# Attention on one core: keys loaded in rows of eight, a first group in pieces, copies as words, and two routes that alternate by unit

## The chip, the cores and the metric

The kernel runs on one core of a Trainium2 chip. The time is device microseconds of one launch; the median of three runs before the change is 1265.33 us (1265.04 to 1265.5). One more execution was taken with the hardware profiler; everything said of stages and engines comes from it.

## The reference

Softmax attention over 512 independent heads (16 x 32), with 192 query rows, 1024 keys and a head width of 128, all in bf16:

```
B, H, Sq, Sk, D = 16, 32, 192, 1024, 128

def reference(q, k, v):
    scale = q.shape[-1] ** -0.5
    scores = jnp.einsum("bhqd,bhkd->bhqk", q, k) * scale
    p = _softmax(scores, axis=-1)
    return jnp.einsum("bhqk,bhkd->bhqd", p, v)
```

K and V are 134.2 MB each, Q and the output 25.2 MB each; all of it passes through the DMA engines once.

## The kernel before

**Tiling.** Heads are taken in groups of 16 (`G`), 32 groups in all. A group is eight pairs of heads, and a pair is three units of 128 query rows: rows 0 to 127 of head a, rows 0 to 127 of head b, and the last 64 rows of both side by side. The third kind of unit (`k3 == 2`) runs as two matmuls of 64 columns on two halves of the array (`tile_position`). There are 24 units in a group and 768 in the program; unit u of the text is u % 3 == k3.

**A unit's way.** TensorE makes the scores of all 1024 keys into PSUM (`s_ps`, L215, or L222 and L228 for the third unit): two matmuls of 512 columns, stationary operand from `qt`, moving operand from `kt`. VectorE copies them, scaled and negated, to `ss` in SBUF and takes the row's extreme on the way (L300). Then one of two routes follows:

- `R_W`: GpSimd subtracts the extreme and writes bf16 to `x_sb` (L188). TensorE transposes `x_sb` in eight blocks (L244) into `pt_ps`. ScalarE applies exp while it copies PSUM to `pt_sb` (L367). No row sum exists then, so TensorE makes it along with P times V: beside each of the eight matmuls with V (L267) stands one with a column of ones (L270), the same stationary operand again.
- `R_EA`: ScalarE applies exp first and accumulates the row sum in the same instruction (L356). TensorE transposes (L244), ScalarE copies PSUM to `pt_sb` unchanged (L369), and P times V needs no ones.

`ROUTES=(R_W, R_W, R_EA)` is indexed by u % 3, so both full units of a pair go by `R_W` and the third, split unit always by `R_EA`; its matmuls with V are L273 and L275, and the lines for ones on the split unit never run.

**Order.** Each engine has its own hand-written program and waits on semaphores. TensorE does in step s: scores of unit s+1, transposes of unit s-4, P times V of unit s-7. Three steps are a pair. `s_ps` and `pt_ps` have two buffers each, `x_sb` four.

**Keys.** `kt` holds K transposed, one key after another; a block of the transpose takes every eighth column, so that block t holds keys t, t+8, t+16 and so on, which is how V lies in `vs` (partition p holds the eight keys 8p to 8p+7, 2 KB in a row):

```
ins = pe.transpose(PT[:, t, :], X[:, t: SK: KT_TILES], ident[:])
```

**Loads and stores.** All DMAs are issued by SyncE (SP), in order, on one queue. For a group: K with a transpose in flight (L141, 4 MB), Q likewise (L144, 0.75 MB), V as it is (L149, 4 MB), and for the output three stores (L158, L163, L164, 0.75 MB). Two groups are held at once. The program's start loads groups 0 and 1; then, for each g, come the loads of g+2 and the stores of g. The load of K waits until the scores of group g are done (`s_qk`), that of V until its P times V is done (`s_pv`), the stores until its last pair is normalised (`s_on`).

Of the kernel before, what the change touches and what calls it, by code (L numbers as in the profile page):

```python
# [5 lines left out]
BF16 = mybir.dt.bfloat16  # L6
F32 = mybir.dt.float32
# [5 lines left out]
R_W = 2  # L13


def _attention_kernel(nc, q, k, v, out, G=16, NS=2, LAGS=(2, 4, 5, 7), ROUTES=(R_W, R_W, R_EA)):
    B, H, SQ, D = q.shape
    SK = k.shape[2]
    assert D == 128 and SK == 1024 and SQ == 192, (D, SK, SQ)
# [43 lines left out]
    with ExitStack() as es:  # L63
# [6 lines left out]
        def sem(name):  # L70
            return es.enter_context(nc.semaphore(name))

        kt = sb("kt", [128, NS, G * SK], BF16)
        qt = sb("qt", [128, NS, G * SQ], BF16)
        vs = sb("vs", [128, NS, G, KT_TILES, 128], BF16)
        ob = sb("ob", [128, NSO, PPG, 4, 128], BF16)
# [5 lines left out]
        rinv = sb("rinv", [128, 2, 4], F32)  # L82
        ones = sb("ones", [128, 128], BF16)
        ident = sb("ident", [128, 128], BF16)
        s_ps = [ps("s_ps%d" % i, [128, SK], F32) for i in range(2)]
        pt_ps = [ps("pt_ps%d" % i, [128, KT_TILES, 128], BF16) for i in range(2)]
        o_ps = [ps("o_ps%d" % i, [128, 4, 128], F32) for i in range(2)]
        s_setup = sem("s_setup")
        sxk = [sem("sxk%d" % i) for i in range(NS)]
        sxq = [sem("sxq%d" % i) for i in range(NS)]  # L90
        svl = [sem("svl%d" % i) for i in range(NS)]
        sst = [sem("sst%d" % i) for i in range(NSO)]
        s_qk = sem("s_qk")
        s_max = sem("s_max")
# [17 lines left out]

        O_SLOT = (0, 2, 1)

        def load_cnt(g):
            return 16 * (g // NS + 1)

        def store_cnt(g):
            return 48 * (g // NSO + 1)
# [12 lines left out]

        @block.sync
        def _(e):
            def loads(g):
                s = g % NS
                last_u = (g - NS + 1) * UPG - 1
                h0 = g * G
                if g >= NS:
                    e.wait_ge(s_qk, last_u + 1)  # L140
                e.dma_start_transpose(  # L141
                    kt[:, s], kf[h0:h0 + G].rearrange("g k d -> (g k) d")
                ).then_inc(sxk[s], 16)
                e.dma_start_transpose(  # L144
                    qt[:, s], qf[h0:h0 + G].rearrange("g k d -> (g k) d")
                ).then_inc(sxq[s], 16)
                if g >= NS:
                    e.wait_ge(s_pv, last_u + 1)
                e.dma_start(  # L149
                    vs[:, s], vf[h0:h0 + G].rearrange("g (p t) d -> p g t d", t=KT_TILES)  # L150
                ).then_inc(svl[s], 16)

            def stores(g):
                so = g % NSO
                e.wait_ge(s_on, (g + 1) * PPG)
                h0 = g * G
                og = of[h0:h0 + G]
                e.dma_start(  # L158
                    og[:, 0:128, :].rearrange("h p d -> p h d"),
                    ob[:, so].rearrange("p pg (x y) d -> p (pg x) (y d)", y=2)[:, :, 0:128],  # L160
                ).then_inc(sst[so], 16)
                oab = og[:, 128:192, :].rearrange("(pg x) p d -> x p pg d", x=2)
                e.dma_start(oab[0], ob[0:64, so, :, 1, :]).then_inc(sst[so], 16)  # L163
                e.dma_start(oab[1], ob[64:128, so, :, 1, :]).then_inc(sst[so], 16)  # L164

            for g in range(min(NS, NGR)):
                loads(g)
            for g in range(NGR):
                if g + NS < NGR:
                    loads(g + NS)  # L170
                stores(g)
            for so in range(min(NSO, NGR)):
                n_uses = len(range(so, NGR, NSO))
                e.wait_ge(sst[so], 48 * n_uses)

        @block.gpsimd
# [21 lines left out]
        def _(pe):  # L198
            def qk(u):
                pr, k3, g, pg = unit_info(u)  # L200
                s = g % NS
                if u % UPG == 0:
                    pe.wait_ge(sxk[s], load_cnt(g))
                    pe.wait_ge(sxq[s], load_cnt(g))
                if u >= 2:
                    pe.wait_ge(s_max, u - 1)
                S = s_ps[u % 2]
                a = 2 * pg
                b = 2 * pg + 1
                ins = None  # L210
                for c in range(2):
                    cs = slice(512 * c, 512 * c + 512)
                    if k3 < 2:
                        x = a if k3 == 0 else b
                        ins = pe.matmul(  # L215
                            S[:, cs],
                            qt[:, s, x * SQ: x * SQ + 128],
                            kt[:, s, x * SK + 512 * c: x * SK + 512 * c + 512],
                            start=True, stop=True,
                        )  # L220
                    else:
                        pe.matmul(  # L222
                            S[0:64, cs],
                            qt[:, s, a * SQ + 128: a * SQ + 192],
                            kt[:, s, a * SK + 512 * c: a * SK + 512 * c + 512],
                            start=True, stop=True, tile_position=(0, 0),
                        )
                        ins = pe.matmul(  # L228
                            S[64:128, cs],
                            qt[:, s, b * SQ + 128: b * SQ + 192],  # L230
                            kt[:, s, b * SK + 512 * c: b * SK + 512 * c + 512],
                            start=True, stop=True, tile_position=(0, 64),
                        )
                ins.then_inc(s_qk, 1)

            def tr(u):
                wait_x(pe, u)
                if u >= 2:
                    wait_evac(pe, u - 2)
                X = x_sb[:, u % NX, :]  # L240
                PT = pt_ps[u % 2]
                ins = None
                for t in range(KT_TILES):
                    ins = pe.transpose(PT[:, t, :], X[:, t: SK: KT_TILES], ident[:])  # L244
                ins.then_inc(s_tr, 1)

            def pv(u):
                pr, k3, g, pg = unit_info(u)
                s = g % NS
                if u % UPG == 0:  # L250
                    pe.wait_ge(svl[s], load_cnt(g))
                wait_evac(pe, u)
                if k3 == 0 and pr >= 2:
                    pe.wait_ge(s_on, pr - 1)
                O = o_ps[pr % 2]
                PTS = pt_sb[:, u % NPT]
                sl = O_SLOT[k3]
                a = 2 * pg
                b = 2 * pg + 1
                ins = None  # L260
                with_rs = route(u) == R_W
                for t in range(KT_TILES):
                    first = t == 0
                    last = t == KT_TILES - 1
                    if k3 < 2:
                        x = a if k3 == 0 else b
                        ins = pe.matmul(O[:, sl, :], PTS[:, t, :], vs[:, s, x, t, :],  # L267
                                        start=first, stop=last, skip_group_check=True)
                        if with_rs:
                            ins = pe.matmul(O[:, 3, sl: sl + 1], PTS[:, t, :], ones[:, 0:1],  # L270
                                            start=False, stop=last, skip_group_check=True)
                    else:
                        pe.matmul(O[0:64, sl, :], PTS[:, t, 0:64], vs[:, s, a, t, :],  # L273
                                  start=first, stop=last, skip_group_check=True, tile_position=(0, 0))
                        ins = pe.matmul(O[64:128, sl, :], PTS[:, t, 64:128], vs[:, s, b, t, :],  # L275
                                        start=first, stop=last, skip_group_check=True, tile_position=(0, 64))
                        if with_rs:
                            pe.matmul(O[0:64, 3, sl: sl + 1], PTS[:, t, 0:64], ones[:, 0:1],
                                      start=False, stop=last, skip_group_check=True, tile_position=(0, 0))
                            ins = pe.matmul(O[64:128, 3, sl: sl + 1], PTS[:, t, 64:128], ones[:, 0:1],  # L280
                                            start=False, stop=last, skip_group_check=True, tile_position=(0, 64))
                ins.then_inc(s_pv, 1)
# [12 lines left out]
        def _(dve):  # L295
            def rowmax(u):
                dve.wait_ge(s_qk, u + 1)
                if u >= NSS:
                    wait_x(dve, u - NSS)
                dve.tensor_scalar(  # L300
                    ss[:, u % NSS, :], s_ps[u % 2][:], -scale, None, ALU.mult, ALU.min,
                    accum_out=nb[:, u % NSS: u % NSS + 1],
                ).then_inc(s_max, 1)

# [43 lines left out]
        def _(act):  # L348
# [13 lines left out]
            def evac(u):  # L362
# [3 lines left out]
                if route(u) == R_W:  # L366
                    act.activation(pt_sb[:, u % NPT], pt_ps[u % 2][:], ACT_FN.Exp, scale=-1.0).then_inc(s_eva, 1)  # L367
                else:
                    act.activation(pt_sb[:, u % NPT], pt_ps[u % 2][:], ACT_FN.Copy).then_inc(s_eva, 1)  # L369

            for step in range(NU + L_EV + 1):
                u = step - L_EV
# [43 lines left out]
```

## Time and profile before

| | us |
|---|---|
| median of three runs | 1265.33 |
| span of the profiled execution (its own time; no other is recorded of it) | 1263.1 |
| TensorE matmul busy | 1234.2 |
| VectorE busy | 1102.0 |
| ScalarE busy | 1048.6 |
| GpSimd busy | 960.4 |
| first score matmul starts | 21.0 |
| last store issued | 1259.06 |

The mean granted TensorE clock is 0.999 of full speed. Busy time of TensorE is not TensorE at its peak: matmuls are pipelined, and their records overlap. The DMA engines moved 321.9 MB, 255 GB/s on average, of which K, Q and the output go in packets of 256 B. The share of the DMA engines in the page's slices stands at nine tenths or more from the first to the 38th of 40 slices. Instructions of the engines are themselves fetched by DMA: 164 packets of 16 KB, one in 7.7 us.

### The profile page before, as it was taken

How to read it: one execution, taken by the hardware profiler on the slowest of the kernel's cores; microseconds unless marked ns; L12 is line 12 of the kernel's file. 1: busy time of each engine (PE TensorE's matmuls, PEld its weight loads, DVE VectorE, ACT ScalarE, POOL GpSimd, SP SyncE). 2: the span in 40 equal slices, each digit the busy share in tenths (PEclk: the TensorE clock that was granted, in tenths of full speed). 3: DMA queues.
4: the chain of work that ended last, by engine and by line, in shares of the span. 5: the costliest groups of instructions: out<-in, count | busy, mean ns of one | idle time of the engine just before them, and what ended most of it. 6: DMA issues, size and time to landing. Idle time of an engine off the chain costs nothing.

```text
span 1263.1 us, 48658 instructions
## 1 busy us (share of the span) xinstructions
PE 1234.2 (98%) x20480; PEld 1009.4 (80%) x20480; DVE 1102.0 (87%) x2304; ACT 1048.6 (83%) x1281; POOL 960.4 (76%) x518
## 2 busy tenths in 40 slices
PE   3999999999999999999999999999999999999997
PEld 1888888888888888888888888888888888888886
DVE  2889888898988989898898988889898898989885
ACT  1888888888888888888888888888888888888886
POOL 2778777777877778787777877777787777878774
PEclk9999999999999999999999999999999999999999
DMA  9999999999999999999999999999999999999941
GB/s 288 268 261 240 278 280 266 288 270 245 254 269 261 279 233 255 281 275 262 261 230 272 271 276 268 252 251 272 272 267 281 253 263 252 271 261 281 244 118 27
DMA packets 790743, 321.89 MB, mean 255 GB/s; under 512 B 724992, under 2 KB 724992, under 8 KB 790528
## 3 DMA queue, kind: packets, MB, share of 16 engines
q1 hardware_dynamic: 790528, 318.78, 108.8%
q8 instruction: 164, 2.69, 0.8%
q14 instruction: 51, 0.42, 0.1%
HBM read 134.22 MB, written 25.17 MB: 126 GB/s over the span
## 4 chain that ended last, share of the span: by engine, by line
PE 97%; SPq 1%; DMA 1%; ACT 0%; issue 0%; DVE 0%; ACTq 0%
PE pt_ps L244 33%; PE o_ps L267 24%; PE s_ps L215 18%; PE o_ps L273 11%; PE s_ps L222 9%; SPq L141 1%; DMA vs<-in_v_dram 1%; PE o_ps L270 1%; PE o_ps L275 1%; SPq L144 0%; PE s_ps L228 0%; ACT x_sb L356 0%; ACT pt_sb L367 0%; DVE ob L330 0%; DVE rinv L327 0%
## 5 line engine op out<-in xcount | busy, mean ns | idle before, releaser
L188 POOL TENSOR_TENSOR x_sb<-ss,nb 128x1024 bf16<-128x1024 f32 x512 | 959.7, 1895 | 288.9 <-PE pt_ps L244 266.8
L300 DVE TENSOR_SCALAR_CACHE_REDUCE ss<-s_ps 128x1024 f32<-128x1024 f32 x768 | 938.5, 1222 | 140.5 <-PE s_ps L215 110.8
L244 PEld LDWEIGHTS pt_ps<-ident,x_sb 128*128 128x128 bf16 x6144 | 487.1, 148 | 203.3 <-issue 105.4
L367 ACT ACTIVATE pt_sb<-pt_ps 128x1024 bf16<-128x1024 bf16 x512 | 521.0, 1018 | 41.9 <-PE pt_ps L244 41.8
L244 PE MATMUL pt_ps<-ident,x_sb 128*128 128x128 bf16 x6144 | 520.7, 228 | 0.2 <-ACT pt_sb L367 0.2
L267 PE MATMUL o_ps<-vs,pt_sb 128*128 128x128 bf16 x4096 | 403.0, 217 | 0.3 <-DMA vs<-in_v_dram 0.3
L369 ACT ACTIVATE pt_sb<-pt_ps 128x1024 bf16<-128x1024 bf16 x256 | 262.1, 1024 | 140.1 <-PE pt_ps L244 140.0
L270 PE MATMUL o_ps<-ones,pt_sb 128*128 128x1 bf16 x4096 | 376.0, 165 | 0.0
L267 PEld LDWEIGHTS o_ps<-vs,pt_sb 128*128 128x128 bf16 x4096 | 352.3, 97 | 0.5 <-DMA vs<-in_v_dram 0.4
L270 PEld LDWEIGHTS o_ps<-ones,pt_sb 128*128 128x128 bf16 x4096 | 340.7, 96 | 0.0
L215 PE MATMUL s_ps<-kt,qt 128*128 128x512 bf16 x1024 | 305.3, 379 | 21.3 <-DMA qt<-in_q_dram 21.0
L356 ACT ACTIVATE x_sb<-ss,nb 128x1024 bf16<-128x1024 f32 x256 | 292.3, 1142 | 23.6 <-DVE ss L300 23.6
L273 PE MATMUL o_ps<-vs,pt_sb 128*64 128x128 bf16 x2048 | 162.3, 222 | 0.0
L275 PE MATMUL o_ps<-vs,pt_sb 128*64 128x128 bf16 x2048 | 162.3, 222 | 0.0
L222 PE MATMUL s_ps<-kt,qt 128*64 128x512 bf16 x512 | 153.2, 381 | 0.6 <-DVE ss L300 0.5
L228 PE MATMUL s_ps<-kt,qt 128*64 128x512 bf16 x512 | 153.2, 381 | 0.0
L330 DVE TENSOR_TENSOR ob<-o_ps,rinv 128x384 bf16<-128x384 f32 x256 | 142.7, 557 | 8.7
L273 PEld LDWEIGHTS o_ps<-vs,pt_sb 128*64 128x64 bf16 x2048 | 121.0, 109 | 17.1
L275 PEld LDWEIGHTS o_ps<-vs,pt_sb 128*64 128x64 bf16 x2048 | 121.0, 109 | 0.0
L215 PEld LDWEIGHTS s_ps<-kt,qt 128*128 128x128 bf16 x1024 | 63.3, 96 | 23.6 <-issue 21.5
L300 DVE DVE_READ_ACCUMULATOR ss<-s_ps 128x1 f32 x768 | 64.0, 83 | 0.0
L356 ACT ACTIVATION_READ_ACCUMULATOR x_sb<-ss,nb 128x1 f32 x256 | 48.9, 191 | 0.0
(11 smaller groups left out, 165.7 us busy)
## 6 DMA issues: line engine op xcount, KB each, us to landing
vs<-in_v_dram SPq DMA_DIRECT2D x32, 4096.0 KB, 15.2
out_dram<-ob SPq DMA_DIRECT2D x32, 512.0 KB, 15.9
out_dram<-ob SPq DMA_DIRECT2D x64, 128.0 KB, 4.9
kt<-in_k_dram SPq DMA_TRANSPOSE x32, 21.4
qt<-in_q_dram SPq DMA_TRANSPOSE x32, 6.6
```

The costliest lines, as they stand in the source:

```text
L188: gp.tensor_tensor(x_sb[:, u % NX, :], ss[:, u % NSS, :], nb[:, u % NSS: u % NSS + 1].to_broadcast([128, SK]), ALU.subtract,).then_inc(s_x ...
L215: ins = pe.matmul(S[:, cs], qt[:, s, x * SQ: x * SQ + 128], kt[:, s, x * SK + 512 * c: x * SK + 512 * c + 512], start=True, stop=True,)
L222: pe.matmul(S[0:64, cs], qt[:, s, a * SQ + 128: a * SQ + 192], kt[:, s, a * SK + 512 * c: a * SK + 512 * c + 512], start=True, stop=True, ...
L244: ins = pe.transpose(PT[:, t, :], X[:, t: SK: KT_TILES], ident[:])
L267: ins = pe.matmul(O[:, sl, :], PTS[:, t, :], vs[:, s, x, t, :], start=first, stop=last, skip_group_check=True)
L270: ins = pe.matmul(O[:, 3, sl: sl + 1], PTS[:, t, :], ones[:, 0:1], start=False, stop=last, skip_group_check=True)
L273: pe.matmul(O[0:64, sl, :], PTS[:, t, 0:64], vs[:, s, a, t, :], start=first, stop=last, skip_group_check=True, tile_position=(0, 0))
L275: ins = pe.matmul(O[64:128, sl, :], PTS[:, t, 64:128], vs[:, s, b, t, :], start=first, stop=last, skip_group_check=True, tile_position=(0, ...
L300: dve.tensor_scalar(ss[:, u % NSS, :], s_ps[u % 2][:], -scale, None, ALU.mult, ALU.min, accum_out=nb[:, u % NSS: u % NSS + 1],).then_inc(s ...
L356: act.activation(x_sb[:, u % NX, :], ss[:, u % NSS, :], ACT_FN.Exp, bias=nb[:, u % NSS: u % NSS + 1], scale=-1.0, accum_out=rs[:, pr % NRS ...
L367: act.activation(pt_sb[:, u % NPT], pt_ps[u % 2][:], ACT_FN.Exp, scale=-1.0).then_inc(s_eva, 1)
L369: act.activation(pt_sb[:, u % NPT], pt_ps[u % 2][:], ACT_FN.Copy).then_inc(s_eva, 1)
```

## The change

Four edits, of which the first has several places:

1. K is read in rows of eight keys. The source of the transpose is seen as 2048 rows of 1024 numbers in place of 16384 rows of 128, and `kt` becomes `[128, NS, 8, G * 128]`: key 8p+t of a head stands at column p of plane t. The score matmul's moving operand is then four planes of 128 keys, and the scores come out with the keys in the order of t, then p. A block of the transpose on TensorE is therefore 128 neighbouring columns of `x_sb`.
2. The routes are `(R_W, R_EA)`: even units go by `R_W`, odd ones by `R_EA`. 384 units go each way, in place of 512 and 256. Of every six units (two pairs), two full units and one split unit go by `R_W`.
3. Group 0 is loaded in pieces of 2, 6 and 8 heads with semaphores of their own, in the order K, Q of heads 0 to 1; K, Q of 2 to 7; V of 0 to 1; V of 2 to 7; K, Q, V of 8 to 15. The last group's output is stored in pieces of 4, 2, 1 and 1 pairs.
4. The copy of the `R_EA` route from `pt_ps` to `pt_sb` sees both as 512 fp32 words in place of 1024 bf16 numbers.

```diff
-def _attention_kernel(..., ROUTES=(R_W, R_W, R_EA)):
+def _attention_kernel(..., ROUTES=(R_W, R_EA),
+                      FIRST=((0, 2), (2, 8), (8, 16)), LAST=((0, 4), (4, 6), (6, 7), (7, 8))):
...
-        kt = sb("kt", [128, NS, G * SK], BF16)
+        kt = sb("kt", [128, NS, KT_TILES, G * 128], BF16)
...
+        def words(t):
+            return t.rearrange("p t q -> p (t q)").bitcast(F32)
...
+            def load_kq(g, a, b, sems):
+                s = g % NS
+                h0 = g * G
+                e.dma_start_transpose(
+                    kt[:, s, :, a * 128:b * 128],
+                    kf[h0 + a:h0 + b].rearrange("g (p t) d -> (g p) (t d)", t=KT_TILES),
+                ).then_inc(sems[0], 16)
...
-                e.dma_start_transpose(
-                    kt[:, s], kf[h0:h0 + G].rearrange("g k d -> (g k) d")
-                ).then_inc(sxk[s], 16)
...
+            n = len(FIRST)
+            for i in range(n):
+                load_kq(0, *FIRST[i], (sf[i], sf[i]))
+                if i > 0:
+                    for i2 in range(i if i > 1 else 0, i + 1):
+                        load_v(0, *FIRST[i2], sfv[i2])
+            for g in range(1, min(NS, NGR)):
                 loads(g)
             for g in range(NGR):
                 if g + NS < NGR:
                     loads(g + NS)
-                stores(g)
+                for a, b in (LAST if g == NGR - 1 else ((0, PPG),)):
+                    stores(g, a, b)
...
+                    def keys(x):
+                        return kt[:, s, cs, x * 128:x * 128 + 128]
...
-                            kt[:, s, x * SK + 512 * c: x * SK + 512 * c + 512],
+                            keys(x),
...
-                    ins = pe.transpose(PT[:, t, :], X[:, t: SK: KT_TILES], ident[:])
+                    ins = pe.transpose(PT[:, t, :], X[:, t * 128:t * 128 + 128], ident[:])
...
-                    act.activation(pt_sb[:, u % NPT], pt_ps[u % 2][:], ACT_FN.Copy).then_inc(s_eva, 1)
+                    act.activation(words(pt_sb[:, u % NPT]), words(pt_ps[u % 2][:]), ACT_FN.Copy).then_inc(s_eva, 1)
```

`load_v` and `stores` issue the same DMAs as before for the heads `a` to `b` of a group. `load_cnt` counts one load less for the groups that share a buffer with group 0. For groups 1 to 31 the loads are one DMA each, in the order and with the waits of before.

## The prediction

> **What bounds the kernel now.** I read the chain of waits first, then TensorE's timeline inside a pair, then SyncE's timeline, because a bound that is nearly reached by a second resource does not show in the chain.
>
> ```profile
> PE 97%; SPq 1%; DMA 1%; ACT 0%; issue 0%; DVE 0%; ACTq 0%
> ```
>
> TensorE alone carries the chain. One pair in the middle, by the starts (columns: start, duration in us):
>
> ```profile
> 600.24 0.59 PE L215 MATMUL s_ps<-kt,qt 128*128 128x512 bf16 x2
> 600.67 0.66 PE L244 MATMUL pt_ps<-ident,x_sb 128*128 128x128 bf16 x8
> 601.16 0.22 PE L267 MATMUL o_ps<-vs,pt_sb 128*128 128x128 bf16 x1
> 601.22 0.17 PE L270 MATMUL o_ps<-ones,pt_sb 128*128 128x1 bf16 x1
> 601.25 0.22 PE L267 MATMUL o_ps<-vs,pt_sb 128*128 128x128 bf16 x1
> ...
> 601.81 0.59 PE L215 MATMUL s_ps<-kt,qt 128*128 128x512 bf16 x2
> 602.83 0.24 PE L273 MATMUL o_ps<-vs,pt_sb 128*64 128x128 bf16 x1
> 603.30 0.38 PE L222 MATMUL s_ps<-kt,qt 128*64 128x512 bf16 x1
> 603.83 0.71 PE L244 MATMUL pt_ps<-ident,x_sb 128*128 128x128 bf16 x8
> 604.38 0.22 PE L267 MATMUL o_ps<-vs,pt_sb 128*128 128x128 bf16 x1
> 605.04 0.59 PE L215 MATMUL s_ps<-kt,qt 128*128 128x512 bf16 x2
> ```
>
> From L215 to the L215 of the next pair are 4.80 us, 38.4 per group of eight pairs. Scores take 0.43 us, eight transposes 0.49 (0.55 behind a split unit), eight matmuls with V and eight with ones 0.65, the split unit's matmuls with V 0.47. To the nanosecond the trace has 55 ns from an L267 to its L270 and 26 from there to the next L267, and 64.5 on average from one L244 to the next.
>
> Now the queue that feeds it (SyncE, same columns):
>
> ```profile
> 595.90 19.96 SPq L141 DMA_TRANSPOSE kt<-in_k_dram  x1
> 615.91 3.94 SPq L144 DMA_TRANSPOSE qt<-in_q_dram  x1
> 619.89 0.59 SPq L149 DMA_DIRECT2D vs<-in_v_dram  x1
> 620.52 5.06 SPq L158 DMA_DIRECT2D out_dram<-ob  x1
> 625.63 9.81 SPq L163 DMA_DIRECT2D out_dram<-ob  x1
> 635.48 1.59 SPq L164 DMA_DIRECT2D out_dram<-ob  x1
> 637.11 17.95 SPq L141 DMA_TRANSPOSE kt<-in_k_dram  x1
> ```
>
> There is no hole: each issue takes as long as the queue needs to drain. From the K of group 4 (140.96) to that of group 26 (978.34) stand 22 periods of 38.06 us, SyncE behind in all of them. So the DMA needs 38.06 us a group and TensorE 38.4. TensorE does not feel it, because loads run ahead: Q of group 16 lands some 6.6 us (its median) after 615.91 and is first used at 633.84. But a TensorE that needs less than 38.06 will meet the queue. The last K is issued at 1170.34, at 1188.00 follows its Q, landing at 1194; only about 5.5 us of the whole way there were waits for TensorE (groups 27 to 29, up to 2.6 us each).
>
> **The change, part by part; TensorE.** (a) Transposes from neighbouring columns. Their weight loads stand out:
>
> ```profile
> L244 PEld LDWEIGHTS pt_ps<-ident,x_sb 128*128 128x128 bf16 x6144 | 487.1, 148 | 203.3 <-issue 105.4
> L267 PEld LDWEIGHTS o_ps<-vs,pt_sb 128*128 128x128 bf16 x4096 | 352.3, 97 | 0.5 <-DMA vs<-in_v_dram 0.4
> ```
>
> Same shape; the strided one takes 148 ns, the unstrided 97. I take 55.5 ns per transpose in place of 64.5, the pace of L267 to L270, which also streams 128 columns: 48 per two pairs x 9 = -0.42 us. Bounds: 0 if the stride is not the cause, -0.45 if all go at 55.
> (b) Ones. Two pairs have four full units with ones now: 4 x 8 x 26 ns = 0.84 us. After, two full units (0.42) and one split unit, whose pairs of ones the trace does not show. Nearest rows: a second half-array matmul starts 3 ns after its partner (L275 after L273), so 26 + 3 = about 30 ns a pair, 0.24; bounds 0, and 8 x 53 = 0.42 if a pair costs a step of L273's. Net -0.18 (-0.42 to 0). The number of matmuls stays 20480, so instruction fetches stay too.
> Two pairs: 9.60 - 0.60 = 9.00 us, 36.0 a group (bounds 34.9 to 38.4).
>
> **The other engines.** ScalarE per six units: before 4 x 1.018 + 2 x 1.024 + 2 x 1.13 (the last from start to start, 599.06 to 600.19) = 8.4 us. After, 3 x 1.018 + 3 x 1.13 + 3 copies. A copy of 512 words is not in the trace: between 0.51 (half of 1.024) and 1.024. I take 0.65, as 128x1024 takes 1018 ns from bf16 and 1142 from fp32, so elements count more than bytes: 8.4 us, under 9.0. At 1.024 it is 9.5, 38.1 a group, above TensorE.
> The Trainium skill, "ScalarE: Activation LUTs", What ACT_TABLE_LOAD costs, gives 186 ns + 0.833 ns per element whatever the type: by it (an estimate) the copy takes 612 ns and ScalarE's sum is 8.3.
> GpSimd goes from 4 x 1.895 to 3 x 1.895 = 5.7 us, nobody's bound. VectorE's instructions are the same: 1102.0/32 = 34.4 us a group, covered while TensorE needs 36; at the low bound of 34.9 it would be as late as TensorE. New waits are only at group 0; behind them TensorE's whole program is queued.
>
> **The DMA.** Same bytes, and the same three loads a group from group 1 on. What changes is that a block of the transpose reads rows 2048 B apart in place of 256 B. K alone, before anything computes (columns: window, its length, busy of the five engines, clock, DMA share, GB/s):
>
> ```profile
> 5.00:10.00 5.00, 0.00 (x0) 0.00 (x0) 0.00 (x0) 0.00 (x0) 0.00 (x0) 1.00 1.28 290
> ```
>
> This is a steady 290 GB/s in packets of 256 B, 18 ns each. The rows are 256 B to the engines either way, so I take 0 us for the change. Bounds: a gain of 1.5 us per K if the interruptions (18 us in the middle against 14.9 for the first K) were halved; a loss, if each of the eight planes pays what a transpose costs at the start: Q's 192 blocks take 3.07 us and K's 1024 14.90, so 14.2 ns a block and 0.34 fixed; 7 x 0.34 = 2.4 us per K.
> The Trainium skill, "DMA: Bandwidth & Descriptors", Latency and other measured facts, speaks against the change: a DMA transpose whose middle dimension is not contiguous ran at 261 GB/s, against 350 to 400 contiguous. This trace's contiguous one has 290 with packets already 256 B, so I do not take the loss. By 261, K would lose 1.6 us and the time be some 1294; by the ratio of 0.7, 6.2 us and some 1436.
>
> **The start.** First K and Q (0.6 MB of 4.75, which end at 21.0) should be there at about 5.3, so TensorE starts 15.7 us earlier. But Q of group 1 lands at 55.8 now, and the same bytes stand before it; group 1 was first used at 57.8. So the pieces buy nothing while the DMA is the bound. They add two changes between transposes and plain loads, which cost 1.5 us each (V 0 landed 12.3 us after Q 0, 4 MB at 400 GB/s are 10.5): +3 us. The pieces of the last output shorten the way from the last matmul to the end from 6.8 to about 5.5.
>
> **The sum.** The DMA paces. The last Q lands at 1194.0 - 5.5 (waits for TensorE gone) + 3 = 1191.5. Then group 31: 36.0 us of scores; from the last score to the end 16.4 us before (1246.7 to 1263.1), 9.2 + 5.5 = 14.7 after. Span 1242.2. The span was 2.2 us under the median of the runs, so 1244.
>
> **Rivals.**
> *TensorE remains the bound* because the queue runs faster once SyncE is never held. For it: groups 4 to 9 took 37.2 us. Against it: 22 periods of 38.06 without a wait. If the DMA needed 36 or less: 1263.1 - 128 x 0.59 - 15.7 - 1.3 + 2.2 = 1173; at 37.2, 1244 - 31 x 0.86 = 1217.
> *ScalarE becomes the bound*, words being as slow as bf16: group 1 at 57.8, 31 x 38.1, and 14.7: 1254 + 2.2 = 1256. For it: 1.024 is the only row of a copy.
> *The rows of eight slow K's transpose* (slower than before): at SyncE's L141, decisive from 0.7 us per K (21 us over 31 groups), since the queue has no slack. With 2.4 us: 1244 + 31 x 2.4 = 1318. For it: nothing in the trace shows a strided transpose. Against it: the constant rate of 290.
> *The change doesn't reach TensorE* (transposes stay at 64.5): 9.42 a two-pair, 37.7 a group, still under 38.06: the same 1244, plus 2.
>
> **How the numbers follow.** DMA pace unchanged (with its sub-cases of TensorE) 0.50, own range 1217 to 1258; ScalarE 0.08; faster queue, down to 1173, 0.14; slower K 0.28, of which half between 1260 and 1320. The range 1200 to 1320 leaves out some 0.06 below and 0.14 above. A change within 0.2% (2.5 us), about what a measurement here can tell from none, has 0.04; slower by more 0.26, faster by more 0.70.
>
> **What would show it.** L244's successor with weight loads near 97 ns and starts 55 apart; a pair of 4.5 us inside a group; TensorE waiting one to two us for `kt` or `qt` at group starts, with L141's successor in 18 us; the copy near 0.65 us. An issue of K over 18.7 us, and 290 GB/s no longer reached before TensorE starts, would make it wrong.

## The result, and the profile after

The changed kernel takes 1262.26 us (median of 20 executions, 1258.03 to 1269.81), the kernel before 1265.54 (20 executions, 1264.81 to 1269.83, in the same comparison). The ratio is 0.9971, with a 95% interval of 0.9959 to 0.9983: faster, by 3.3 us, where 21 were forecast. The profiled execution of after took 1258.7 us and has a span of 1256.9; it is 3.6 us quicker than the median of its kernel.

First the chain of waits of after, shares of the span by engine:

```profile
PE 81%; DMA 11%; SPq 4%; issue 3%; ACT 0%; DVE 0%
```

TensorE had 97% of it before. The rest has gone to transfers and to the queue that issues them, so the bound has moved where the forecast put it. TensorE's waits in after (waiting line, what released it, us in total, times, longest):

```profile
PEld s_ps L248 <- issue: 60.2, 31, 6.8
PE s_ps L248 <- issue: 48.6, 25, 6.6
PE s_ps L248 <- DMA qt<-in_q_dram: 14.1, 3, 6.8
```

L248 is the first score matmul of a unit. It now stands idle 31 times by its weight load's count, about once a group, and the trace has the landing of Q about 0.1 us before the group's first score in 25 of the 28 groups from 4 on. "Issue" here is a wait for two semaphores that the view did not put down to a transfer.

SyncE's timeline, one group in the last third (start, duration):

```profile
990.46 17.41 SPq L144 DMA_TRANSPOSE kt<-in_k_dram  x1
1007.91 4.66 SPq L148 DMA_TRANSPOSE qt<-in_q_dram  x1
1012.61 0.59 SPq L155 DMA_DIRECT2D vs<-in_v_dram  x1
1013.25 4.92 SPq L174 DMA_DIRECT2D out_dram<-ob  x1
1018.21 9.73 SPq L179 DMA_DIRECT2D out_dram<-ob  x1
1027.98 0.63 SPq L180 DMA_DIRECT2D out_dram<-ob  x1
1028.65 18.38 SPq L144 DMA_TRANSPOSE kt<-in_k_dram  x1
```

There is no hole, as before. This group takes 38.2 us; from the K of group 4 (145.06) to that of group 31 (1183.1) stand 27 periods of 38.45 us, against 38.12 before. The queue did not get quicker when TensorE stopped holding it; it got slower by 0.3 us a group.

TensorE's own instructions went as they were costed. The groups of after (instructions, busy us and mean ns, idle before):

```profile
L277 PEld LDWEIGHTS pt_ps<-ident,x_sb 128*128 128x128 bf16 x6144 | 390.6, 98 | 231.5 <-issue 61.5
L404 ACT ACTIVATE pt_sb<-pt_ps 128x1024 bf16<-128x1024 bf16 x384 | 393.2, 1024 | 184.4 <-PE pt_ps L277 184.4
L406 ACT ACTIVATE pt_sb<-pt_ps 128x512 f32<-128x512 f32 x384 | 225.4, 587 | 39.3 <-PE pt_ps L277 39.0
```

The weight load of a transpose block is 98 ns (148 before), and the copy as words 587 ns beside the 1024 of the exp (L404) from the same buffer. By the Trainium skill, "ScalarE: Activation LUTs", What ACT_TABLE_LOAD costs, the copy would be 612 ns, an estimate; the trace is 4% under that. Ones on a split unit, from TensorE's timeline of after:

```profile
1011.00 0.24 PE L312 MATMUL o_ps<-vs,pt_sb 128*64 128x128 bf16 x1
1011.07 0.17 PE L315 MATMUL o_ps<-ones,pt_sb 128*64 128x1 bf16 x1
1011.08 0.17 PE L317 MATMUL o_ps<-ones,pt_sb 128*64 128x1 bf16 x1
1011.10 0.22 PE L310 MATMUL o_ps<-vs,pt_sb 128*64 128x128 bf16 x1
```

From L315 to the next L310 are 0.03 us: a pair of ones on two halves costs about 30 ns, as taken. From a group's first score to its last now pass 35.0 us at the least and 35.5 on average (36.9 before).

### The profile page after: what moved, and what is told of

It is laid out like the page before. It is cut to its first block, busy times and chain, and to the rows that moved or that the text cites. A ratio compares the mean times of both kernels' runs of the same rounds, so it can differ in the third digit from the quotient of the medians.

```text
span 1256.9 us, 48804 instructions
## 1 busy us (share of the span) xinstructions
PE 1185.2 (94%) x20480; PEld 917.6 (73%) x20480; DVE 1102.4 (88%) x2304; ACT 1017.6 (81%) x1537; POOL 728.6 (58%) x390
## 4 chain that ended last, share of the span: by engine, by line
PE 81%; DMA 11%; SPq 4%; issue 3%; ACT 0%; DVE 0%
PE pt_ps L277 26%; PE o_ps L304 19%; PE s_ps L248 16%; PE o_ps L310 11%; PE s_ps L255 8%; DMA vs<-in_v_dram 7%; DMA kt<-in_k_dram 4%; SPq L144 2%; SPq L148 2%; PE o_ps L312 0%; PE o_ps L307 0%; PE o_ps L317 0%; SPq L155 0%; PE s_ps L261 0%; ACT x_sb L393 0%
## 5 line engine op out<-in xcount | busy, mean ns | idle before, releaser
L213 POOL TENSOR_TENSOR x_sb<-ss,nb 128x1024 bf16<-128x1024 f32 x384 | 727.9, 1896 | 516.4 <-PE pt_ps L277 508.1
L277 PEld LDWEIGHTS pt_ps<-ident,x_sb 128*128 128x128 bf16 x6144 | 390.6, 98 | 231.5 <-issue 61.5
L404 ACT ACTIVATE pt_sb<-pt_ps 128x1024 bf16<-128x1024 bf16 x384 | 393.2, 1024 | 184.4 <-PE pt_ps L277 184.4
L393 ACT ACTIVATE x_sb<-ss,nb 128x1024 bf16<-128x1024 f32 x384 | 438.0, 1141 | 8.2 <-DVE ss L337 8.2
L248 PE MATMUL s_ps<-kt,qt 128*128 128x512 bf16 x1024 | 310.2, 385 | 62.7 <-issue 48.6
L406 ACT ACTIVATE pt_sb<-pt_ps 128x512 f32<-128x512 f32 x384 | 225.4, 587 | 39.3 <-PE pt_ps L277 39.0
L310 PE MATMUL o_ps<-vs,pt_sb 128*64 128x128 bf16 x2048 | 192.7, 225 | 0.0
L312 PE MATMUL o_ps<-vs,pt_sb 128*64 128x128 bf16 x2048 | 192.7, 225 | 0.0
L307 PE MATMUL o_ps<-ones,pt_sb 128*128 128x1 bf16 x2048 | 190.6, 166 | 0.0
L310 PEld LDWEIGHTS o_ps<-vs,pt_sb 128*64 128x64 bf16 x2048 | 154.0, 110 | 27.0 <-issue 1.0
L307 PEld LDWEIGHTS o_ps<-ones,pt_sb 128*128 128x128 bf16 x2048 | 171.8, 96 | 0.3 <-issue 0.3
L312 PEld LDWEIGHTS o_ps<-vs,pt_sb 128*64 128x64 bf16 x2048 | 154.0, 110 | 0.1
L248 PEld LDWEIGHTS s_ps<-kt,qt 128*128 128x128 bf16 x1024 | 70.7, 98 | 68.5 <-issue 60.2
L315 PE MATMUL o_ps<-ones,pt_sb 128*64 128x1 bf16 x1024 | 99.8, 167 | 0.0
L317 PE MATMUL o_ps<-ones,pt_sb 128*64 128x1 bf16 x1024 | 99.8, 167 | 0.0
```

The lines of the kernel that those rows point to most:

```text
L213: gp.tensor_tensor(x_sb[:, u % NX, :], ss[:, u % NSS, :], nb[:, u % NSS: u % NSS + 1].to_broadcast([128, SK]), ALU.subtract,).then_inc(s_x ...
L248: ins = pe.matmul(S[:, cs], qt[:, s, x * SQ:x * SQ + 128], keys(x), start=True, stop=True,)
L277: ins = pe.transpose(PT[:, t, :], X[:, t * 128:t * 128 + 128], ident[:])
L393: act.activation(x_sb[:, u % NX, :], ss[:, u % NSS, :], ACT_FN.Exp, bias=nb[:, u % NSS: u % NSS + 1], scale=-1.0, accum_out=rs[:, pr % NRS ...
L406: act.activation(words(pt_sb[:, u % NPT]), words(pt_ps[u % 2][:]), ACT_FN.Copy).then_inc(s_eva, 1)
```

## The experiments

All were timed against the kernel before on the same chip; its median was 1264.9 to 1265.5 in each comparison. Line numbers in lines shown of an experiment are those of its own program.

**old_rows** undoes the first edit in the changed kernel: K as 16384 rows, strided transposes.

```diff
-    kf[h0 + a:h0 + b].rearrange("g (p t) d -> (g p) (t d)", t=KT_TILES),
+    kf[h0 + a:h0 + b].rearrange("g k d -> (g k) d"),
...
-    ins = pe.transpose(PT[:, t, :], X[:, t * 128:t * 128 + 128], ident[:])
+    ins = pe.transpose(PT[:, t, :], X[:, t: SK: KT_TILES], ident[:])
```

> The changed kernel with K loaded as before (16384 rows of 128) and the strided transposes of before; routes, pieces and word copies stay. Theory (the DMA paces, and K in rows of eight costs the DMA nothing): TensorE needs 37.7 us a group, still under the 38.4 of the DMA; time 1259 to 1266, K's issue 18.0 to 18.3 us. Rival (the rows of eight cost the queue the 0.3 to 0.4 us a group by which the changed kernel's period exceeds 38.06): K's issue back under 18.0 us, time 1250 or less.

Measured: 1268.52 us (1260.78 to 1271.15, 7 executions), ratio 1.0007 (0.9982 to 1.0032). The period is 38.39 us, K's issue 18.17 (after: 18.20), TensorE needs 36.4 us from first to last score. So the longer period is there without rows of eight: they are not what slows the queue. The median is above the 1259 to 1266 that were expected: three executions took 1260.8 to 1262.3, four 1268.5 to 1271.2, and why they fall in two bunches is not known.

**no_v** is the changed kernel without the loads of V from group 2 on; P times V goes on with the V of groups 0 and 1. **before_no_v** does the same to the kernel before.

```diff
-                if g >= NS:
-                    e.wait_ge(s_pv, last_u + 1)
-                load_v(g, 0, G, svl[s])
+                if g < NS:
+                    load_v(g, 0, G, svl[s])
...
```

> The changed kernel without the loads of V from group 2 on; P times V reads the old V, so the output is not attention. Theory (the DMA paces): with 4 MB of 9.5 gone the queue needs some 25 us a group, TensorE paces at 36.0: 1165 to 1185. Rival (something else than the DMA holds TensorE at group starts, such as a wait on VectorE or ScalarE): stays above 1230.

> The kernel before with the same loads of V left out; output not attention. Theory (before, TensorE paced at 38.4 us a group and the DMA was hidden): no change beyond the start, 1255 to 1266. Rival (the DMA paced before too): under 1245.

Measured: 1199.19 us and 1265.98, one execution each. The chain of no_v:

```profile
PE 94%; SPq 2%; DMA 2%; issue 0%; ACT 0%; DVE 0%
```

With 126 MB of transfers gone the changed kernel is bound by TensorE again, at 36.24 us a group (forecast: 36.0), and 63 us shorter; the kernel before does not move. So DMA bounds the one and not the other. The time is still 14 us or more above what was expected, because group 1 begins at 59.6 us there (58.4 in after): starting earlier on group 0 is lost again at group 1, whose Q comes behind everything else. An estimate that subtracts the earlier start (15.7 us) from the end, as the first rival of the prediction did, is too low by about that much.

**stores_act** issues the stores of groups 0 to 30 from ScalarE in place of SyncE, all three in one place; **stores_spread** issues them from ScalarE one at a time, five units apart; **stores_pool** issues all from GpSimd. The last three lines shown are those of stores_spread.

```diff
-                for a, b in (LAST if g == NGR - 1 else ((0, PPG),)):
-                    stores(g, a, b)
+                if g == NGR - 1:
+                    for a, b in LAST:
+                        stores(e, g, a, b)
...
+                g, r = divmod(step - UPG - L_PV - 3, UPG)
+                if r in (0, 5, 10) and 0 <= g < NGR - 1:
+                    stores(act, g, 0, PPG, (r // 5,))
```

> The changed kernel with the output stores of groups 0 to 30 issued by ScalarE in place of SyncE. Theory (the bound is the DMA's time, and part of it is lost between the kinds of transfer on one queue): stores run beside the loads, 0.5 to 2 us a group gained, 1200 to 1250. Rival (the 16 engines have no idle time to gain, every byte costs the same wherever it is issued): 1256 to 1266. Second rival (ScalarE is held by its waits for the stores): above 1270.

> The changed kernel with the output stores of groups 0 to 30 issued by ScalarE, one of the three at a time, five units apart. Theory (the period of 38.4 us is the time of SyncE's queue, and a third of what the stores take there is change-over and waiting in line, not bytes): loads alone need some 36 us, TensorE paces with 36.2, 1195 to 1225. Rival (the engines' bytes are the bound wherever they are issued): 1255 to 1266. ScalarE held as when all three were issued at once: 1270 or more.

> The changed kernel with all output stores issued by GpSimd. Same theory: 1195 to 1225 if GpSimd, which is 58% busy, issues them without holding its subtractions. Rival (bytes are the bound): 1255 to 1266. If GpSimd is held: more.

Measured: stores_act 1281.01 us (1278.44 to 1285.64), ratio 1.0125 (1.01 to 1.0151); stores_spread 1241.32 (1239.98 to 1247.6), 0.9815 (0.979 to 0.9841); stores_pool 1249.47 (1238.31 to 1258.29), 0.9893 (0.9855 to 0.9932). ScalarE's timeline of stores_act shows why the first fails:

```profile
625.44 0.39 ACTq L143 DMA_DIRECT2D out_dram<-ob  x1
625.86 4.19 ACTq L148 DMA_DIRECT2D out_dram<-ob  x1
...
630.08 0.66 ACTq L149 DMA_DIRECT2D out_dram<-ob  x1
630.83 1.02 ACT L405 ACTIVATE pt_sb<-pt_ps 128x1024 bf16<-128x1024 bf16 x1 [4.09 <-issue]
```

The second issue holds ScalarE 4.19 us here (median 3.1, up to 7.0), and TensorE waits for its copies: Q landed 11 to 14 us before it was used. With five units between the issues that is gone (0.64 us for the second issue), and the period falls to 37.7 us, 0.7 less than after. That is far less than the 15 us that the issue of the stores takes of a period on SyncE, which is why 1195 to 1225 had been expected: most of that time is bytes, which have to pass wherever they are issued. They are mostly V's: by the landings in after, V takes 12.7 us of a period and the three stores 3.4.

**no_ones** leaves out the 4096 matmuls with ones (L307, L315, L317), the row sums of their units being set to 1. It tests two things: whether TensorE's load of work matters, and whether its instructions do, which are themselves fetched by DMA.

```diff
-    with_rs = route(u) == R_W
+    with_rs = False
...
```

> The changed kernel without the 4096 matmuls with ones; the row sums of the R_W units are left out (1.0 stands for them), so the output is not attention. TensorE has a fifth fewer instructions to fetch. Theory (a fetch of 16 KB during a transpose in flight stops the transfer for 1.2 to 1.5 us, and 3.4 of 5.1 fetches a group fall there): 33 fetches less, 1 us a group, 1225 to 1240. Rival (the fetches cost only their own bytes, the DMA's period is the same without them): 1256 to 1266, TensorE only waiting longer.

Measured: 1239.03 us (1236.97 to 1242.9), ratio 0.9791 (0.977 to 0.9813). Its queue of instruction fetches (packets, MB, share) and its chain:

```profile
q8 instruction: 132, 2.16, 0.7%
...
PE 55%; DMA 34%; SPq 6%; issue 4%; ACT 0%; DVE 0%; ACTq 0%
```

Against after there are 32 packets of 16 KB fewer (164 there) and the time is 23 us less, 0.7 us a packet, though TensorE now waits some 1 to 4 us in every group (2.6 to 5.3 us from a group's last score to the next one's first, of which 1.2 are there without a wait). A faster TensorE can't be the cause, since TensorE was not the bound; fewer matmuls mean fewer fetches, and the queue's period falls from 38.45 to 37.86.

How a fetch does it shows in the transposes. Windows of 1.2 us of after inside the K that is issued at 608.22 (window, length, busy of the five engines, clock, DMA share, GB/s):

```profile
611.60:612.80 1.20, 1.20 (x26) 0.79 (x23) 1.14 (x6) 0.80 (x3) 0.17 (x1) 1.00 1.27 290
612.80:614.00 1.20, 1.20 (x19) 0.96 (x17) 1.20 (x3) 1.11 (x2) 1.00 (x1) 1.00 1.33 304
614.00:615.20 1.20, 1.20 (x24) 0.96 (x22) 1.01 (x2) 1.20 (x3) 0.90 (x1) 1.00 2.26 107
615.20:616.40 1.20, 1.20 (x29) 0.92 (x26) 1.10 (x1) 0.99 (x2) 0.55 (x1) 1.00 0.52 113
616.40:617.60 1.20, 1.20 (x25) 0.96 (x22) 1.17 (x6) 1.20 (x2) 1.20 (x1) 1.00 1.27 290
...
621.20:622.40 1.20, 1.20 (x19) 1.01 (x18) 1.18 (x2) 0.71 (x2) 0.34 (x1) 1.00 1.97 176
622.40:623.60 1.20, 1.20 (x23) 1.06 (x22) 1.20 (x3) 1.20 (x2) 1.20 (x1) 1.00 0.50 106
623.60:624.80 1.20, 1.20 (x22) 0.86 (x20) 0.91 (x3) 0.99 (x3) 0.36 (x1) 1.00 1.27 290
```

The packet records have fetches of 16 KB at 613.99 and 621.44, and at both the rate falls from 290 to near 110 GB/s for about 2 us. (By the packets it stands near 10 GB/s from 0.5 to 1.75 us after the start of a fetch, on average over those inside K.) Taking what is missing against 290 GB/s in the 3 us after each fetch, over all fetches inside the K of groups 4 to 31, a fetch costs 1.4 us (49 of them). In the same way against 400 GB/s, a fetch inside a load of V costs 0.1 us (27). Another explanation would be that the running engines slow the transposes throughout, by their own traffic with the memory; but where no fetch is near, K moves 290 GB/s (the median of such microseconds) with the engines at work, as it does before anything computes.

**more_fetch** adds fetches on GpSimd: 26 more waits behind each subtraction, which are satisfied already and are 13 instructions in the trace.

```diff
                 if route(u) == R_W:
                     shift(u)
+                    for i in range(26):
+                        gp.wait_ge(s_setup, 1 + i % 2)
```

> The changed kernel with 13 semaphore instructions more on GpSimd before each of 384 subtractions, all satisfied, so GpSimd has some 5000 instructions more to fetch and no other work. Theory (fetches stop the transposes): 39 fetches of 8 KB more, 10 to 40 us, 1272 to 1300. Rival (fetches are free): 1256 to 1266, as GpSimd has time to spare.

Measured: 1264.43 us (1258.86 to 1275.46, 10 executions), ratio 0.9992 (0.9968 to 1.0017). The other instruction queue (q14) has 92 packets in place of 53, of 8 KB, and the period is 38.41. The expected 10 us or more can't be seen. Yet the packet records don't clear GpSimd's fetches: in the 2 us after such a fetch inside K with no fetch of TensorE near it, 0.6 us are missing against 290 GB/s on average (13 of them here, 7 in after, 0.4 to 0.9 us each). So they stop the transposes too, for less time. Some 21 of the extra fetches fall between the landing of the last store and that of Q in groups 4 to 31, where they should add some 0.4 us a period (21 x 0.6 / 28); that stretch is 22.4 us here and 22.3 in after. Why their loss doesn't show in the period is open.

**dma_only** keeps every load and store and their order, and computes nothing (zeros are stored); **dma_only_old** is the same with K as 16384 rows.

> The changed kernel's loads and stores alone: the same DMAs in the same order on SyncE, each load waiting only for the loads of two groups before; nothing is computed, and zeros are stored. Theory (what stretches the queue's period from about 34 to 38.4 us is TensorE's instruction fetches, about 1 us each): K and Q take 18 us as before anything computes, V and stores 16, 34 a group, 1085 to 1115. Rival (the queue needs 38 us for these bytes by itself): 1215 or more.

> The same with K read as before, 16384 rows of 128. Theory (rows of eight cost the queue nothing): within 4 us of its sister run. Rival (rows of eight cost 0.3 us a group): at least 8 us faster than it.

Measured: 1082.76 and 1080.5 us, one execution each. A group of dma_only on SyncE:

```profile
600.84 15.34 SPq L144 DMA_TRANSPOSE kt<-in_k_dram  x1
616.22 3.53 SPq L148 DMA_TRANSPOSE qt<-in_q_dram  x1
619.79 0.59 SPq L155 DMA_DIRECT2D vs<-in_v_dram  x1
...
635.25 15.52 SPq L144 DMA_TRANSPOSE kt<-in_k_dram  x1
```

The mean period is 33.37 us, with old rows 33.34: rows of eight cost the queue 0.03 us a group. And the queue by itself is 5.1 us a group quicker than in after. By the landings, K and Q (from the landing of the last store before them to that of Q) take 22.3 us in after and 18.3 here, so 4.0 of the 5.1 lie there; V and the stores have 0.6 and 0.5 more. In after 84 of TensorE's fetches fall into these stretches in 28 groups; 84 x 1.4 / 28 = 4.2 us a group, about what the transposes lose (with the 26 of GpSimd there at 0.6 it would be 4.8, so the prices of single fetches don't add up in full). In no_ones the stretch takes 21.5 us, with 66 fetches.

**rows_only** puts rows of eight and the unstrided transposes, and nothing else, into the kernel before.

```diff
-    kt[:, s], kf[h0:h0 + G].rearrange("g k d -> (g k) d")
+    kt[:, s], kf[h0:h0 + G].rearrange("g (p t) d -> (g p) (t d)", t=KT_TILES)
...
-    ins = pe.transpose(PT[:, t, :], X[:, t: SK: KT_TILES], ident[:])
+    ins = pe.transpose(PT[:, t, :], X[:, t * 128:t * 128 + 128], ident[:])
```

> The kernel before with K in rows of eight and unstrided transposes alone; routes, copies and whole-group loads as before. Theory (any edit that takes TensorE below 38.4 us a group meets the DMA): TensorE needs 36.7, time 1256 to 1268, the same as with both edits. Rival (TensorE's savings count each by itself): 256 pairs x 0.21 = 54 us less, 1210.

Measured: 1249.36 us (1245.71 to 1253.05), ratio 0.9865 (0.9845 to 0.9885). This was expected to equal the two kernels and is 13 us faster than the whole change. So the rest of the change gives time back. On this chip more_fetch, the whole change plus idle instructions, had 1264.4.

**best1**, tried as the best version then known: the whole change, stores spread on ScalarE, the last group loaded in pieces as the first is, and routes `(R_W, R_W, R_EA, R_W, R_EA, R_EA)`.

> The changed kernel with three more edits: stores issued by ScalarE one at a time (as in the run before); the last group loaded in the same pieces as the first, so that TensorE need not wait for all of it; and routes W, W, EA, W, EA, EA, which keep the halves equal but spend ones on three full units of six in place of two full and one split, 1024 matmuls fewer. Theory: 1241 less some 14 (TensorE begins the last group when 2 of its 16 heads are there) less some 6 (8 fetches): 1215 to 1230. Rival (the chain's end is set elsewhere): 1236 or more.

Measured: 1249.08 us (1243.8 to 1251.75), ratio 0.9868 (0.9849 to 0.9886): worse than stores_spread, though TensorE has 8 fetches fewer (156). Why it is worse is not shown. The pieces of group 31 gain nothing, since TensorE is still at group 30 until 1198.7, which could only begin when its Q landed at 1162.6.

**What the rest of the change gives back** was the question of the last six. **whole_first** undoes the pieces of the first group, **old_routes** undoes the routes and the copy as words, **whole_old_routes** undoes both (left are rows of eight and the last output in pieces), and **rows_only2** is rows_only once more.

```diff
-                      FIRST=((0, 2), (2, 8), (8, 16)), LAST=...
+                      FIRST=((0, 16),), LAST=...
...
```

```diff
-    ROUTES=(R_W, R_EA),
+    ROUTES=(R_W, R_W, R_EA),
...
-    act.activation(words(pt_sb[:, u % NPT]), words(pt_ps[u % 2][:]), ACT_FN.Copy)
+    act.activation(pt_sb[:, u % NPT], pt_ps[u % 2][:], ACT_FN.Copy)
```

> The whole change, but the first group loaded whole: K, Q, V of all 16 heads, in the order of before. The kernel with rows of eight alone took 1249.4 us, the whole change 1262.3, though both wait for the DMA; this and the next kernel each undo one part of what stands between them. Theory 1, the pieces at the start cost it: they made the load of group 4 start 2.8 us later (145.1 against 142.3), and a queue that never has slack keeps that, so this one takes at least 3 us off and, if the period of 38.45 us is a consequence of the start, up to 13: 1249 to 1259. Theory 2, the routes and the copy as words cost it (TensorE needs 35.0 us in place of 35.4 in a group, waits longer, and bunches its instruction fetches): this one stays at 1262, at best 3 us less. Theory 3, scatter from one execution to the next: both stand anywhere between 1249 and 1262, with the executions of one kernel as far apart as the kernels.

> The whole change, but with the routes of before (two units in three by GpSimd's way, the split unit always by ScalarE's) and the copy of bf16 numbers; rows of eight and the first group in pieces stay. Theory 1 (pieces at the start cost the 13 us): 1260 to 1265, like the whole change. Theory 2 (routes and words cost them): 1249 to 1253, K's load near 38.27 us a period. TensorE needs about 36.7 us a group here, still under the queue.

> Both parts undone at once: the first group loaded whole, and the routes and the copy of before; left of the change are rows of eight and the last output in pieces. Each part undone alone gave 1258.1 (whole first group) and 1261.9 (routes), against 1262.3 for the whole change and 1249.4 for rows of eight alone. If the two parts add up: 1257 to 1258, and the 1249.4 was the scatter of four executions. If they act together (each by itself is enough to hold the queue back): 1246 to 1252, as rows of eight alone, less the 1.3 us that the last output in pieces is worth.

> Rows of eight alone once more, the same program as the one that took 1249.4 (1245.7 to 1253.1). If that was scatter: 1255 to 1260. If it is the kernel's time: 1246 to 1253.

| kernel | us (lowest to highest) | ratio, 95% | K of group 4 issued | period, groups 4 to 31 |
|---|---|---|---|---|
| the change | 1262.26 (1258.03 to 1269.81) | 0.9959 to 0.9983 | 145.1 | 38.45 |
| whole_first | 1258.06 (1253.92 to 1258.86) | 0.9922 to 0.9948 | 142.8 | 38.51 |
| old_routes | 1261.89 (1256.10 to 1271.11) | 0.9958 to 0.9994 | 149.7 | 38.50 |
| whole_old_routes | 1247.75 (1244.04 to 1255.96) | 0.9843 to 0.9890 | 140.8 | 38.21 |
| rows_only | 1249.36 (1245.71 to 1253.05) | 0.9845 to 0.9885 | 142.3 | 38.27 |
| rows_only2 | 1248.01 (1246.57 to 1250.21) | 0.9852 to 0.9877 | 142.1 | 38.03 |

Undoing one of the two parts gives back 4.2 us or 0.4, undoing both 14.5. Neither theory of a single culprit holds, nor that it was scatter: 1248 to 1249 came three times. The first-group pieces cost 2 to 9 us at the start, by the fourth column (the four kernels that load the first group whole stand at 140.8 to 142.8). The longer period is there with either part and gone only without both; but each period is from one profiled execution, and rows_only and rows_only2, which are the same program, differ by 0.24 us.

The landings say where it is. K and Q together, from the landing of the last store to that of Q, take 22.3, 22.3 and 22.4 us in the change, whole_first and old_routes, and 21.8, 21.9 and 21.9 in whole_old_routes, rows_only and rows_only2; V differs by less than 0.2 between the six, and the stores take 0.1 to 0.3 less in the first three. So the transposes are what takes longer. Of TensorE's fetches 84, 85 and 85 fall into these stretches in the first three, 82 in each of the others. At 1.4 us, 2 or 3 more in 28 groups make 0.1 to 0.15 us a group, less than the 0.4 to 0.6 seen. Why it takes both parts to be undone is not settled. These kernels ran on several chips, on which the kernel before agreed within 0.7 us.

A group on SyncE in rows_only2, and its chain:

```profile
599.81 18.11 SPq L141 DMA_TRANSPOSE kt<-in_k_dram  x1
617.96 3.99 SPq L144 DMA_TRANSPOSE qt<-in_q_dram  x1
...
637.83 17.69 SPq L141 DMA_TRANSPOSE kt<-in_k_dram  x1
```

```profile
PE 94%; DMA 2%; issue 2%; SPq 1%; ACT 0%; DVE 0%; ACTq 0%
```

This is the forecast's own queue: 38.0 us from K to K, with TensorE (35.4 us from first to last score, 36.8 with the step to the next group) only just under it.

**whole_spread** and **rows_spread** put the spread stores on the two: whole_spread is whole_first with the stores on ScalarE, rows_spread has the routes and the copy of before as well.

> The whole change with the first group loaded whole and the output stores of groups 0 to 30 issued by ScalarE, one at a time, five units apart. The same stores with the first group in pieces took 1241.3 us. Theory 1 (pieces cost at least 3 us at the start): 1230 to 1238. Theory 2 or 3: 1239 to 1246.

> As the kernel before this one (whole first group, stores spread on ScalarE), but with the routes and the copy of before; so rows of eight, the stores on ScalarE and the last output in pieces remain. TensorE needs 36.7 to 36.9 us a group against a period of 37.7, so it is covered by little, and ScalarE has 8.4 us of 9.2 in two pairs and the issues of the stores besides. Theory 2 (routes and words cost the queue time): 1230 to 1238, under whole_spread. Theory 1: within 3 us of whole_spread. A rival: TensorE or ScalarE, with so little cover, falls behind the queue, 1245 to 1255.

Measured, on one chip: 1240.22 us (1236.03 to 1245.7), ratio 0.98 (0.9781 to 0.982), and 1238.2 (1236.92 to 1239.26), ratio 0.9783 (0.9771 to 0.9796). They are within the 3 us of each other that the theory of the pieces allowed, the second 2 us ahead and steadier. But whole_spread misses the 1230 to 1238 expected of it: loading the first group whole gains 1 us on stores_spread, on another chip. With the stores on ScalarE the routes and the copy as words don't lengthen the period either: it is 37.56 us in whole_spread, 37.75 in rows_spread and 37.72 in stores_spread. The chain of rows_spread:

```profile
PE 95%; issue 2%; SPq 1%; DMA 1%; DVE 0%; ACT 0%; ACTq 0%
```

rows_spread beats both kernels: 2.2% under before, 24 us under the change. It keeps of the change the rows of eight and the last output in pieces.

## Why the prediction was wrong

The direction, the new bound and TensorE's terms were right; the size was not. The forecast's span was 1242.2, the measured one 1256.9. Of the 14.7 us between, 1.1 are the start, 14.2 the 27 periods from the K of group 4 to that of group 31, 0.3 the landing of the last Q, and -0.9 the way from there to the end. Another 3.6 us are the distance between the profiled execution and the median.

- *Transposes from neighbouring columns*, 55.5 ns forecast: 57.1 measured on average, start to start, with the stretches of lower clock, and 56 in the median (64.6 and 62 before); weight loads 98 ns. Right.
- *Ones*, 30 ns a pair on the split unit: right. Together 36.0 us a group were forecast, and 36.24 measured in no_v, where TensorE alone sets the pace.
- *ScalarE*, 0.65 us for the copy as words: 0.587. It did not become the bound; that rival is out.
- *Rows of eight cost the DMA nothing*: right. The period with DMA alone differs by 0.03 us; the rival that put 2.4 us on each K is out. The Trainium skill, "DMA: Bandwidth & Descriptors", Latency and other measured facts, would have had the transpose at 261 GB/s; between fetches it ran at 290 here, as with the contiguous rows before.
- *The start*: the pieces buy nothing, as said (the first score starts at 6.8, where 5.3 was taken, but group 1 is first used at 58.4, 57.8 before). The K of group 4 comes 4.1 us later where 3 were forecast; whole_first, without the pieces, has 1.9 of that too. The 1.5 us for a change between transposes and plain loads are less than the prediction's own row, 12.3 - 10.5 = 1.8. The price was only counted there; the last experiments show that this part also has a share in the period.
- *The failed step is the sum's* "The last Q lands at 1194.0 - 5.5 (waits for TensorE gone) + 3 = 1191.5". It treats the queue as something that TensorE can delay but not slow, so that a TensorE out of the way leaves at most the old period and hands back the waits: 27 periods of 37.9 us. Measured are 38.45, and the last Q lands at 1207.1. Two things went wrong in this term. The 5.5 us are more than the prediction's own row gives back: at its 38.06 without a wait, the 27 periods are 1027.6 us, 1.8 under the 1029.4 before. That is 3.7 of the 14.2 us; the other 10.5 are the rise from 38.06 to 38.45. The queue's pace is not its own: alone it needs 33.4 us, the other 5 come while TensorE runs, some 4 of them in the transposes, which its instruction fetches stop. The prediction looked at these ("interruptions") only as a bound on a possible gain of K, and from the unchanged number of instructions took it that their cost stays.
- With rows of eight alone the step nearly holds in one of two executions: rows_only2 needs 1026.7 us for the 27 periods (1029.4 before, 1023.9 forecast), so 2.7 of the 5.5 us came back; rows_only, the same program, needs 1033.4. Their kernel takes 1248 to 1249. What the forecast missed by the other 13 us or so is that the routes, the words and the pieces, none of which has a DMA of its own after the start, make the kernel that much slower while the stores are on SyncE (by 3 us with the stores on ScalarE, on other chips): at the start, and by 0.2 to 0.5 us a period, which lie in the transposes. That they do is shown by undoing them; by what means they lengthen the period is open.
- *TensorE remains the bound* (1173 to 1217) is out by the waits at L248; *the change doesn't reach TensorE* is out by these 57 ns.

## What to carry to other kernels

When an engine's work is cut until a DMA queue paces the kernel, the queue's period of before is no safe price for after: measure the queue with nothing computing, see what the running engines add to it, and look at what changes in that. Cuts that pay then are those in the queue's own time (stores issued elsewhere, spread so that no issue blocks an engine) and in instruction counts, not in TensorE's time. And pieces at the start buy nothing where the next group stands behind the same bytes.

## What the runs showed of the hardware

- TensorE's instruction fetches (164 packets of 16 KB) cost a DMA transpose in flight 1.4 us each and a plain load 0.1. GpSimd's packets of 8 KB cost the transpose some 0.6 us each by the packet records of after and more_fetch, though 39 more of them did not lengthen the kernel measurably.
- A second store issued right behind the first held the issuing ScalarE 3.1 us (median), up to 7.0.
- After some waits of 2 us and more TensorE is granted less clock. Before group 26 of after it stands idle for 2.9 us, from 1013.3 on (windows, same columns as above):

```profile
1011.00:1016.00 5.00, 2.31 (x54) 1.73 (x52) 2.81 (x7) 3.57 (x6) 2.68 (x2) 1.00 1.11 228
1016.00:1021.00 5.00, 4.75 (x56) 3.60 (x56) 2.29 (x3) 1.18 (x2) 0.47 (x1) 0.66 1.02 373
1021.00:1026.00 5.00, 5.00 (x93) 3.70 (x90) 4.82 (x14) 4.56 (x8) 3.31 (x2) 1.00 1.06 388
```

The clock (the column after the busy times) is 0.66 in the window in which it starts again, and that group took 36.6 us from first to last score in place of 35.0. The next group still began 0.1 us after its Q had landed, so here it cost nothing. The one longer wait from group 4 on (4.5 us, from 361.3 on) was followed by a lower clock too; of the five waits of 2.1 to 2.3 us two were and three were not.
